# Fused attention and expert layers on one core: the second token group's first expert products as 2x2 blocks with seven block products

## The chip, the cores and the metric

One core of one Trainium2 chip runs the whole program. The metric is the device time of one execution in microseconds (us), a median over runs. Engine names are those of the profile: PE is TensorE's matmul, PEld its weight load, DVE is VectorE, ACT is ScalarE, POOL is GpSimd, SP is SyncE, whose queue issues nearly all DMAs.

## The reference, cut to what matters

```python
x = attention(q, k, v, tau)                       # 2 x 576 tokens, 8 heads of 64: 1152 x 512
h = np.maximum(np.maximum(x @ w1, x @ w2), x @ w3) # "max" layer, 512 -> 768
x = h @ w_out                                      # 768 -> 512
p = domain_probs / (domain_probs.sum(-1, keepdims=True) + 1e-09)
for e in range(4):                                 # every token goes through every expert
    h = np.maximum(x @ w1[e], 0.0)                 # first expert product, 512 -> 1024
    out += p[:, e:e + 1] * (h @ w2[e])             # second expert product, 1024 -> 512
```

All is float32. The kernel works each product from two-part values: every operand is cut into a high part (rounded to the type that PE multiplies quickly) and a low part (the rest), and a product is the sum of three matmuls, high x low, low x high and high x high.

## The kernel before, in words

The 1152 tokens are two groups: group 0 has 512 tokens, group 1 has 640 (`GROUPS`, line 78), the latter worked as two halves of 320 columns (`subs`). For each group `layer_max` (line 723) runs the max layer and the output product, then `experts` (line 793) the four experts. Both only plan: `add` (line 719) appends a task, which is one PSUM tile, its chain of matmuls, and the functions that read the tile afterwards. `plan.cols` counts the matmul columns planned so far; it is the clock of the plan.

`Stream.run` (line 852) writes the plan out. It issues the matmuls of the tasks one after the other (the matmul is line 859 for all of them), taking the PSUM tile from the pool `mo["ps"]`, which has 3 banks. The readers of a task go out 1000, 2000, ... columns after its end (`AFTER`, line 862). Weight loads and cuts are hooks, put in with `plan.at` at a number of columns ahead of their use (their lag); `flush` (line 843) writes out whatever is due, late functions and hooks in the order of their columns. In the last two regions of the program the order on PE, DVE, ACT and POOL is just this written order (`ORDER_B`, `ORDER_C`), so every engine takes its instructions strictly in turn; that of SP is left to the scheduler.

In the stage of the change, `experts(1)`, each expert is done in two halves of four hidden blocks of 128 (so eight halves). For each block f, `block` (line 644) loads a 128 x 512 weight tile (line 658, 256 KB), cuts its high part on ACT (line 650) and its low part on POOL (line 654). Two tasks (one per 320-column half of the tokens) follow, each of 4 chunks of the 512 inputs times three matmuls; the readers are `hi` (ACT, line 809: relu and rounding) and `lo` (DVE, line 812: relu less the high part, from PSUM). Then five tasks, one per 128 tokens, do the second product: 4 hidden blocks times three matmuls of 512 columns, and `total` (DVE, line 828; line 826 for the first) adds p times the result to the accumulator. The last half stores it (line 786).

The output product of `layer_max(1)` just before makes the inputs `Y[1][d]` (d = 0 to 3, high and low), with `hi` on ACT (line 768) and `lo` on DVE (line 771); for each d the left half of the tokens comes ahead of the right.

Between the groups, at the column count `END0`, group 0's last readers are written out, the pools of the second attention half are closed, and new pools for group 1's hidden tiles and accumulators are opened (lines 959 to 965). The three PSUM banks go on being used.

Of the kernel before, what the change touches and what calls it, by code (L numbers as in the profile page):

```python
# [21 lines left out]
def fused_kernel(ctx: ExitStack, tc: tile.TileContext, q, k, v, tau, w1, w2, w3, w_out, probs, m_w1, m_w2, out):  # L22
    nc = tc.nc
    B, H, S, D = q.shape
    NT, DM = out.shape
    DFF = w1.shape[1]
    E, _, F2 = m_w1.shape
    P = 128
# [6 lines left out]
    KC = DM // P  # L35
# [36 lines left out]
    def f32(ap):  # L72
        return ap.bitcast(F32)
# [3 lines left out]
    N1 = NT - MAIN  # L77
# [2 lines left out]
    cst = ctx.enter_context(tc.tile_pool(name="cst", bufs=1))  # L80
    wp = ctx.enter_context(tc.tile_pool(name="wp", bufs=1))
    dp = ctx.enter_context(tc.tile_pool(name="dp", bufs=1, space=bass.MemoryType.DRAM))
    with tc.using_default_side("right"):
        xp1 = ctx.enter_context(tc.tile_pool(name="xp1", bufs=1))
        xp0 = ctx.enter_context(tc.tile_pool(name="xp0", bufs=1))

    ident = cst.tile([P, P], F32, name="ident")
    make_identity(nc, ident)
# [12 lines left out]
    Y = [[None] * KC for _ in range(2)]  # L101
# [12 lines left out]
    def atile(shape, dt, tag):  # L114
        return at["pool"].tile(shape, dt, tag=tag, name=tag, bufs=at["bufs"].get(tag, 1))
# [337 lines left out]
    class Queue:  # L453
# [3 lines left out]
        def add(self, gen):  # L457
            self.q.append(gen)
# [183 lines left out]
    plan = Plan()  # L642
# [80 lines left out]
    def layer_max(g):  # L723

        G = GROUPS[g]
        hs = [None] * NF
        acc = {}

        def after_max(f, i, si, a, z):
            def first(ps):  # L730
                if hs[f] is None:
                    hs[f] = (htile(g, "hh"), htile(g, "hl"))
                new = wtile([P, z - a], F32, "hmax", 3)
                if i == 0:
# [24 lines left out]
        for d in range(KC):  # L759
            bs = []  # L760
            for i in range(2):
                src = block64(w_out[i * K2 * P:(i + 1) * K2 * P], slice(d * P, (d + 1) * P))
                bs.append(weights64(g, f"o{d}_{i}", plan.cols + i * 3 * K2 * G["subs"][0][1], src, [P, K2, P]))
            for a, z in G["subs"]:
                def hi(ps, d=d, a=a, z=z):
                    if Y[g][d] is None:
                        Y[g][d] = tuple((xp0, xp1)[g].tile([P, G["n"]], F32R, tag="xy", name=f"y{g}{part}{d}", bufs=2 * KC) for part in "hl")
                    nc.scalar.activation(out=Y[g][d][0][:, a:z], in_=ps, func=AF.Copy)

                def lo(ps, d=d, a=a, z=z):  # L770
# [22 lines left out]
    def experts(g):  # L793

        G = GROUPS[g]
        FH = NF2 // 2
        nt = G["n"] // P
        accs = {}
        for e in range(E):
            for half in range(2):  # L800
                hs = [None] * FH
                for f in range(FH):
                    c0 = (half * FH + f) * P
                    b = block(plan.cols, [P, KC, P], "a", NA, None, lags(G, LAGS_A[e + half > 0][f]), src=m_w1[e, :, c0:c0 + P].rearrange("(k p) f -> p k f", p=P))
# [12 lines left out]
                ws = []  # L817
                for f in range(FH):
                    r0 = (half * FH + f) * P
                    ws.append(block(plan.cols, [P, DM], "b", NB, None, lags(G, LAGS_B[f]), src=m_w2[e, r0:r0 + P, :]))  # L820
                for t in range(nt):
                    def total(ps, t=t, e=e, half=half):
                        pe = pr[:, G["c0"] + t, e:e + 1]
                        if e == 0 and half == 0:
                            accs[t] = mo["acc"].tile([P, DM], F32, tag="acc", name="acc", bufs=nt)
                            nc.vector.tensor_scalar(out=accs[t], in0=ps, scalar1=pe, scalar2=None, op0=ALU.mult)
                        else:
                            nc.vector.scalar_tensor_tensor(out=accs[t], in0=ps, scalar=pe, in1=accs[t], op0=ALU.mult, op1=ALU.add)  # L828
# [4 lines left out]
                    add(DM, FH, lambda f, ts=ts, hs=hs, ws=ws: (  # L833
                        hs[f][0][:, ts], hs[f][1][:, ts], ws[f]["hi"], ws[f]["lo"]), [total])

    class Stream:

# [93 lines left out]
        pass  # L931
    stage.close()

    def open_experts(name, side):
        with tc.using_default_side(side):
            mo["h"] = ctx.enter_context(tc.tile_pool(name=f"hp{name}", bufs=1))
            mo["acc"] = ctx.enter_context(tc.tile_pool(name=f"accp{name}", bufs=1))

    region.close()
    region = ordered(ORDER_B)  # L940
    mo["ps"] = ctx.enter_context(tc.tile_pool(name="psM", bufs=3, space=PSUM))
    mo["bits"] = words_pool.enter_context(tc.tile_pool(name="bitsp", bufs=2, space=PSUM))
    open_experts(0, "right")
    while stream.now < QUE0:
        next(products)
    for before, until in (("turned", QUE1), ("valued", QUE2)):
# [52 lines left out]
```

## Time and profile before, and how to read it

| what | value |
|---|---|
| median of 3 runs | 738.38 us (738.06 to 738.91) |
| the profiled execution | 738.01 us, of which the span from first to last instruction is 736.2 us |
| PE busy | 707.0 us of the span |
| POOL, DVE, ACT busy | 377.2, 379.6, 324.8 us |
| instructions | 11651, of them 4047 matmuls |
| mean granted clock | 0.995 of full speed |

Busy time of PE is not its peak: matmuls are pipelined, so a matmul that is shown with 0.31 us may start 0.15 us after the one before. The distance from start to start tells what one costs. "Idle before" is the time in which an engine had nothing running, and the arrow behind it names what ended it.

### The profile page before, as it was taken

Reading aid. Unit: us, or ns where it says so; the run is one execution under the profiler, and the core shown is the slowest. Engines: PE = TensorE matmul, PEld = TensorE weight load, DVE = VectorE, ACT = ScalarE, POOL = GpSimd, SP = SyncE. Lnnn points to the kernel's source line nnn. Section 1 sums busy time; section 2 is a strip of 40 time slices with the busy share of each in tenths; the row PEclk is TensorE's granted clock in tenths of the full one; section 3 lists DMA queues with packets and bytes.
Section 4 is the critical chain, followed back from the end, with each engine's and each line's share of the span. In section 5 each row is a group of like instructions: output and inputs, shape, how many; then the busy total and the mean of one; then the engine's idle time right before and its main releaser. Section 6 shows DMA issues by size and latency. Waiting matters only on the chain.

```text
span 736.2 us, 11651 instructions
## 1 busy us (share of the span) xinstructions
PE 707.0 (96%) x4047; PEld 629.3 (85%) x4047; DVE 379.6 (52%) x907; ACT 324.8 (44%) x681; POOL 377.2 (51%) x394
## 2 busy tenths in 40 slices
PE   5988899999999999999999999999999999999997
PEld 3877789777888888878888899999998998998995
DVE  6898898775476676666676311212222222222222
ACT  5777875544554564454454323234331321322320
POOL 4778876776563564564465344455423423523520
PEclk9899999999999999999999999999999999999999
DMA  6644606877766246153222322224412312312303
GB/s 185 156 96 103 181 1 193 268 220 223 195 164 167 72 109 163 58 135 104 60 85 58 115 76 72 76 66 115 115 49 66 115 46 70 115 44 71 115 1 71
DMA packets 95150, 80.86 MB, mean 110 GB/s; under 512 B 26356, under 2 KB 75764, under 8 KB 95092
## 3 DMA queue, kind: packets, MB, share of 16 engines
q1 hardware_dynamic: 94642, 79.83, 39.9%
q8 instruction: 32, 0.52, 0.3%
q10 hardware_dynamic: 418, 0.30, 0.2%
q14 instruction: 26, 0.21, 0.1%
q0 software_dynamic: 32, 0.00, 0.0%
HBM read 59.53 MB, written 8.65 MB: 93 GB/s over the span
## 4 chain that ended last, share of the span: by engine, by line
PE 80%; DVE 7%; ACT 3%; POOL 3%; issue 3%; DMA 2%; SPq 0%; DVEq 0%; ACTq 0%; POOLq 0%
PE ps L859 67%; PE u L434 4%; PE s L317 4%; PE t L358 3%; DVE em L340 2%; DMA words<-in_moe_w_dram 1%; POOL a L654 1%; DVE st_negm L328 1%; ACT em L335 1%; POOL b L683 1%; DMA krem<-in_k_dram 1%; DVE raw L691 1%; POOL hl L745 1%; DVE hmax L737 1%; ACT a L650 1%
## 5 line engine op out<-in xcount | busy, mean ns | idle before, releaser
L654 POOL TENSOR_TENSOR a<-raw,a 128x512 fp32r<-128x512 f32 (+1 forms) x116 | 145.1, 1257 | 170.5 <-ACT a L650 162.5
L859 PE MATMUL ps<-b,hh 128*128 128x512 f32 x576 | 184.9, 393 | 0.0
L859 PEld LDWEIGHTS ps<-b,hh 128*128 128x128 f32 x576 | 107.4, 188 | 20.8 <-POOL b L654 0.4
L859 PE MATMUL ps<-b,hl 128*128 128x512 f32 x288 | 113.1, 393 | 0.0
L859 PE MATMUL ps<-y1h,a 128*128 128x320 f32 x512 | 112.8, 309 | 0.0
L809 ACT ACTIVATE hh<-ps 128x320 fp32r<-128x320 f32 (+1 forms) x96 | 46.9, 488 | 147.1 <-PE ps L859 146.8
L654 POOL TENSOR_TENSOR b<-raw,b 128x512 fp32r<-128x512 f32 x64 | 82.9, 1296 | 56.2 <-ACT b L650 56.2
L812 DVE SCALAR_TENSOR_TENSOR hl<-ps,hh 128x320 fp32r<-128x320 f32 (+1 forms) x96 | 53.5, 557 | 102.6 <-ACT hh L809 102.4
L650 ACT ACTIVATE a<-raw 128x512 fp32r<-128x512 f32 (+1 forms) x116 | 69.5, 612 | 66.7 <-DVE raw L691 20.7
L828 DVE SCALAR_TENSOR_TENSOR acc<-ps,pr,acc 128x512 f32<-128x512 f32 x63 | 47.2, 749 | 77.7 <-PE ps L859 77.5
L859 PEld LDWEIGHTS ps<-y1h,a 128*128 128x128 f32 x512 | 85.4, 188 | 0.3
L859 PE MATMUL ps<-y0h,a 128*128 128x512 f32 x256 | 84.1, 399 | 0.0
L335 ACT ACTIVATE em<-s,st_negm 128x576 f32<-128x576 f32 x72 | 53.4, 743 | 68.9 <-DVE st_negm L328 66.2
L348 POOL TENSOR_SCALAR em<-em,st_r,even 128x576 f32<-128x576 f32 x70 | 57.7, 825 | 48.2 <-DVE st_r L347 34.2
L859 PE MATMUL ps<-y1l,a 128*128 128x320 f32 x256 | 79.1, 309 | 0.0
L328 DVE TENSOR_REDUCE st_negm<-s 128x1 f32<-128x576 f32 x72 | 54.2, 754 | 45.7 <-PE s L317 45.6
L859 PE MATMUL ps<-x1h,a 128*128 128x320 f32 x288 | 63.4, 309 | 0.0
L859 PEld LDWEIGHTS ps<-b,hl 128*128 128x128 f32 x288 | 54.1, 188 | 10.0
L340 DVE SCALAR_TENSOR_TENSOR em<-s,st_thr,em 128x576 f32<-128x576 f32 x72 | 58.4, 812 | 6.6 <-ACT em L335 4.4
L317 PE MATMUL s<-K,QS 128*128 128x288 f32 x264 | 49.8, 313 | 7.4 <-DVE em L340 6.9
L859 PEld LDWEIGHTS ps<-y0h,a 128*128 128x128 f32 x256 | 47.3, 189 | 8.4
L317 PEld LDWEIGHTS s<-K,QS 128*128 128x128 f32 x264 | 41.9, 197 | 12.8 <-issue 5.7
(128 smaller groups left out, 1241.5 us busy)
## 6 DMA issues: line engine op xcount, KB each, us to landing
raw<-in_moe_w_dram SPq DMA_DIRECT2D x128, 256.0 KB, 2.8
words<-in_moe_w_dram SPq DMA_DIRECT2D x18, 512.0 KB, 6.2
kept_w<-raw SPq DMA_DIRECT2D x18, 256.0 KB, 2.5
raw<-kept_w SPq DMA_DIRECT2D x18, 256.0 KB, 2.6
K<-KN SPq DMA_DIRECT2D x14, 288.0 KB, 5.0
K<-KN SPq DMA_DIRECT2D x14, 256.0 KB, 3.5
words<-in_moe_w_out_dram SPq DMA_DIRECT2D x8, 384.0 KB, 4.9
vnat<-in_v_dram SPq DMA_DIRECT2D x8, 256.0 KB, 4.4
```

Of the source, the lines that this page charges most:

```text
L317: nc.tensor.matmul(st.s[:, kh, 0:HS], lhsT=l, rhs=r, start=i == 0, stop=i == len(terms) - 1)
L328: nc.vector.tensor_reduce(out=st.stat["negm"], in_=views(st)[0], op=ALU.max, axis=AX.XY, negate=True)
L335: return nc.scalar.activation(out=ev, in_=sv, func=AF.Exp, bias=st.stat["negm"])
L340: nc.vector.scalar_tensor_tensor(out=ev, in0=sv, scalar=st.stat["thr"], in1=ev, op0=ALU.is_ge, op1=ALU.mult, accum_out=st.stat["sum"])
L348: last = (nc.vector if swift else nc.gpsimd).tensor_scalar(out=em, in0=em, scalar1=re, scalar2=even, op0=ALU.mult, op1=ALU.add)
L434: at["valued"] = nc.tensor.matmul(pv, lhsT=l, rhs=r, start=i == 0, stop=i == len(terms) - 1)
L650: nc.scalar.activation(out=b["hi"], in_=b["raw"], func=AF.Copy)
L654: nc.gpsimd.tensor_tensor(out=b["lo"], in0=b["raw"], in1=f32(b["hi"]), op=ALU.subtract)
L809: nc.scalar.activation(out=hs[f][0][:, a:z], in_=ps, func=AF.Relu)
L812: nc.vector.scalar_tensor_tensor(out=hs[f][1][:, a:z], in0=ps, scalar=0.0, in1=f32(hs[f][0][:, a:z]), op0=ALU.max, op1=ALU.subtract)
L828: nc.vector.scalar_tensor_tensor(out=accs[t], in0=ps, scalar=pe, in1=accs[t], op0=ALU.mult, op1=ALU.add)
L859: nc.tensor.matmul(ps, lhsT=l, rhs=r, start=i == 0, stop=i == count - 1)
```

## The change

The eight block products of each pair of hidden blocks become seven. The inputs are split into a low half (d = 0, 1) and a high half (d = 2, 3), the pair of hidden blocks into two, the tokens into left and right: a 2x2 by 2x2 block product, done in Winograd's form of Strassen's method. It needs four sums of weight blocks and four sums of input blocks.

- Input sums (`mixed_values`): the readers of the output product of `layer_max(1)` also make the four mixed inputs `BT`, high and low, on DVE and ACT. For d = 2 and 3 the right half of the tokens now comes first.
- Weight sums (`pair_block`): one load of 512 KB per pair takes the place of two of 256 KB. Four sums on DVE (two functions, `sums` and `sums2`), three cuts on ACT and three on POOL, each with its own lag. The buffers are doubled.
- Products (`mixed_pair`): seven tasks per pair, each of 2 chunks times three matmuls of 320 columns. Their readers add the seven results up on DVE, and then do relu, high and low. For two of the four outputs ("calm") relu and high are on ACT and low is on POOL.
- The second products take the token tiles in the order 4 to 0, and the hidden blocks as 0, 1, 3, 2.
- Pools: group 0's input pool and its hidden, accumulator and PSUM pools are closed at `END0`; group 1 gets a new PSUM pool of 8 banks and a pool `mixp`.

```diff
+    group0 = ExitStack()
...
-        xp0 = ctx.enter_context(tc.tile_pool(name="xp0", bufs=1))
+        xp0 = group0.enter_context(tc.tile_pool(name="xp0", bufs=1))
...
-            for a, z in G["subs"]:
+            for a, z in G["subs"] if d < KC // 2 else G["subs"][::-1]:
...
-                    bs[j // K2]["hi"][:, j % K2, :], bs[j // K2]["lo"][:, j % K2, :], hs[j][0][:, a:z], hs[j][1][:, a:z]), [hi, lo])
+                    bs[j // K2]["hi"][:, j % K2, :], bs[j // K2]["lo"][:, j % K2, :], hs[j][0][:, a:z], hs[j][1][:, a:z]),
+                    [hi, lo] if g == 0 else mixed_values(d, a > 0, hi, lo))
...
+    def mixed_values(d, right, hi, lo):
...
+        y0, y1, t2, t3 = (lambda nm=nm, x=x: whole(nm)[:, x, :] for nm in "yt" for x in range(2))
+        if low and not right:
+            return [hi, lo, keep(0)]
+        if low:
+            return [less(y0, y0), *cut(0, y0), keep(1)]
+        if right:
+            return [less(y0, t2), less(y1, t3), *cut(1, t2), *cut(2, t3), hi, lo]
+        return [less(t2, t2), *cut(3, t2), hi, lo]
+
+    def pair_block(use, src, lags):
...
+            b["raw"] = mo["mix"].tile([P, KC, 2 * P], F32, tag="wraw", name="wraw", bufs=2)
+            nc.sync.dma_start(out=b["raw"], in_=src)
...
+            nc.vector.tensor_tensor(out=S(0), in0=raw(1, 0), in1=raw(1, 1), op=ALU.add)
+            nc.vector.tensor_tensor(out=S(2), in0=raw(0, 0), in1=raw(1, 0), op=ALU.subtract)
...
+            nc.vector.tensor_tensor(out=S(1), in0=S(0), in1=raw(0, 0), op=ALU.subtract)
+            nc.vector.tensor_tensor(out=S(3), in0=raw(0, 1), in1=S(1), op=ALU.subtract)
...
+        for fn, lag in zip((load, sums, sums2, hi, shi(0), shi(2), lo, slo(0), slo(2)), lags):
+            plan.at(use - lag, fn)
...
+    LAGS_PAIR = (
+        (44000, 30000, 29000, 28000, 27000, 26000, 26500, 24000, 21500),
+        (44000, 29000, 28000, 27000, 26000, 25000, 24000, 21500, 18500))
+
+    def mixed_pair(b, hs, f):
...
+            def lo(ps):
+                if calm:
+                    nc.gpsimd.tensor_tensor(out=hs[f + i][1][:, cols], in0=val[nm], in1=f32(hs[f + i][0][:, cols]), op=ALU.subtract)
+                else:
+                    nc.vector.scalar_tensor_tensor(
+                        out=hs[f + i][1][:, cols], in0=val[nm], scalar=0.0, in1=f32(hs[f + i][0][:, cols]), op0=ALU.max, op1=ALU.subtract)
...
+        for w, y, after in (
+                (lambda: d(0), direct(0, left), [copy("cx")]),
+                (lambda: s(0), mixed(0), [keep("p5")]),
+                (lambda: s(1), mixed(1), [plus("cu", "cx"), plus("cv", "cu", "p5")]),
+                (lambda: s(2), mixed(2), [plus("cw", "cv"), plus("cu", "cu"), *act(1, right, "cw", True)]),
+                (lambda: d(1), direct(1, left), [plus("cx", "cx"), *act(0, left, "cx", True)]),
+                (lambda: s(3), direct(1, right), [plus("cv", "cv"), *act(0, right, "cv")]),
+                (lambda: d(2), mixed(3), [plus("cu", "cu"), *act(1, left, "cu")])):
+            add(TH, KC // 2, lambda j, w=w, y=y: tuple(t[:, j, :] for t in w()) + tuple(y(j)), after)
...
-                for f in range(FH):
+                for f in range(0, FH, 2) if g == 1 else ():
+                    c0 = (half * FH + f) * P
+                    b = pair_block(plan.cols, m_w1[e, :, c0:c0 + 2 * P].rearrange("(k p) f -> p k f", p=P), LAGS_PAIR[f // 2])
+                    mixed_pair(b, hs, f)
+                for f in range(FH) if g == 0 else ():
...
-                for t in range(nt):
+                for t in range(nt)[::1 if g == 0 else -1]:
...
+                    add(DM, FH, lambda i, ts=ts, hs=hs, ws=ws, order=(0, 1, 2, 3) if g == 0 else (0, 1, 3, 2): (
...
-    open_experts(1, "left")
+    group0.close()
+    open_experts(1, "left", ctx)
+    mo["ps"] = ctx.enter_context(tc.tile_pool(name="psN", bufs=8, space=PSUM))
+    mo["mix"] = ctx.enter_context(tc.tile_pool(name="mixp", bufs=1))
```

## Rows read from the trace of the kernel before

**Rows 1.** The chain that ended last, its last pieces: start us, us, what.

```profile
413.18 318.36 PE ps L859 x1878
731.54 0.02 issue
731.56 0.75 DVE acc L828
```

**Rows 2.** Busy time by stretch: max layer of group 1, its experts, one half of these.

```profile
core 0: us, PE busy (x) PEld busy (x) DVE busy (x) ACT busy (x) POOL busy (x), PEclk, DMA share, GB/s
425.10:509.76 84.66, 84.66 (x579) 84.62 (x578) 16.00 (x32) 27.38 (x58) 40.91 (x38) 1.00 0.26 76
509.76:731.54 221.78, 221.76 (x1250) 202.53 (x1248) 61.24 (x104) 60.23 (x126) 80.25 (x63) 1.00 0.27 75
537.50:565.20 27.70, 27.70 (x158) 25.34 (x157) 7.69 (x13) 7.77 (x16) 10.25 (x8) 1.00 0.26 76
```

**Rows 3.** The timeline of the first expert task's end: start us, us, what.

```profile
511.08 0.31 PE L859 MATMUL ps<-y1l,a 128*128 128x320 f32 x1
511.22 0.46 PE L859 MATMUL ps<-y1h,a 128*128 128x320 f32 x2
511.52 0.31 PE L859 MATMUL ps<-y1l,a 128*128 128x320 f32 x1
511.72 0.44 ACT L809 ACTIVATE hh<-ps 128x320 fp32r<-128x320 f32 x1 [0.80 <-PE ps L859]
```

**Rows 4.** The timeline of group 0's last matmuls and of what follows them.

```profile
424.15 0.39 PE L859 MATMUL ps<-b,hl 128*128 128x512 f32 x1
424.37 0.62 PE L859 MATMUL ps<-b,hh 128*128 128x512 f32 x2
424.83 0.39 PE L859 MATMUL ps<-b,hl 128*128 128x512 f32 x1
425.28 0.30 PE L859 MATMUL ps<-x1l,a 128*128 128x320 f32 x1
425.48 0.75 DVE L828 SCALAR_TENSOR_TENSOR acc<-ps,pr,acc 128x512 f32<-128x512 f32 x1 [1.97 <-PE ps L859]
```

**Rows 5.** Groups by line and shape, 509.76 to 731.54: xcount | busy us, mean ns | idle before.

```profile
L859 PE MATMUL ps<-y1h,a 128*128 128x320 f32 x512 | 112.8, 309 | 0.0
L859 PE MATMUL ps<-y1l,a 128*128 128x320 f32 x256 | 79.1, 309 | 0.0
L654 POOL TENSOR_TENSOR b<-raw,b 128x512 fp32r<-128x512 f32 x32 | 41.6, 1301 | 28.5 <-ACT b L650 28.5
L654 POOL TENSOR_TENSOR a<-raw,a 128x512 fp32r<-128x512 f32 x31 | 39.5, 1294 | 100.5 <-ACT a L650 100.5
L812 DVE SCALAR_TENSOR_TENSOR hl<-ps,hh 128x320 fp32r<-128x320 f32 x64 | 31.5, 492 | 82.6 <-ACT hh L809 82.6
L809 ACT ACTIVATE hh<-ps 128x320 fp32r<-128x320 f32 x64 | 27.8, 435 | 137.5 <-PE ps L859 137.5
L828 DVE SCALAR_TENSOR_TENSOR acc<-ps,pr,acc 128x512 f32<-128x512 f32 x34 | 25.5, 751 | 65.7 <-PE ps L859 65.7
L650 ACT ACTIVATE a<-raw 128x512 fp32r<-128x512 f32 x30 | 17.3, 626 | 9.8 <-PE ps L859 9.8
```

**Rows 6.** Groups by shape on DVE and POOL, whole span: other shapes.

```profile
L218 DVE TENSOR_TENSOR em<-qnat,em 128x256 f32<-128x256 f32 x2 | 0.8, 419 | 0.0
L745 POOL TENSOR_TENSOR hl<-hmax,hh 128x320 fp32r<-128x320 f32 x12 | 10.6, 880 | 22.1 <-ACT hh L742 22.1
L451 POOL TENSOR_TENSOR x0l<-x,x0h 128x256 fp32r<-128x256 f32 x7 | 5.2, 737 | 0.5 <-ACT x0h L448 0.4
L654 POOL TENSOR_TENSOR a<-raw,a 128x384 fp32r<-128x384 f32 x16 | 16.3, 1019 | 14.5 <-ACT a L650 14.4
```

**Rows 7.** The timeline near 105 us: a DVE and a POOL instruction, both on SBUF.

```profile
103.89 1.28 POOL L409 TENSOR_TENSOR am<-tcopy,am 128x512 fp32r<-128x512 f32 x1
104.98 0.58 DVE L348 TENSOR_SCALAR em<-em,st_r,even 128x576 f32<-128x576 f32 x1
```

**Rows 8.** DMA issues: xcount, KB each, median us from issue to landing.

```profile
raw<-in_moe_w_dram SPq DMA_DIRECT2D x128, 256.0 KB, 2.8
words<-in_moe_w_dram SPq DMA_DIRECT2D x18, 512.0 KB, 6.2
```

More of the change, by code (lines that the diff above doesn't have):

```diff
@@ L773, in layer_max, with part, whole, keep @@
                 add(z - a, NF, lambda j, bs=bs, a=a, z=z: (
-                    bs[j // K2]["hi"][:, j % K2, :], bs[j // K2]["lo"][:, j % K2, :], hs[j][0][:, a:z], hs[j][1][:, a:z]), [hi, lo])
+                    bs[j // K2]["hi"][:, j % K2, :], bs[j // K2]["lo"][:, j % K2, :], hs[j][0][:, a:z], hs[j][1][:, a:z]),
+                    [hi, lo] if g == 0 else mixed_values(d, a > 0, hi, lo))
+    TH = N1 // 2
+    BT = [[None] * KC for _ in range(4)]
+    full = {}
+    def mixed_values(d, right, hi, lo):
+        low, c = d < KC // 2, d % (KC // 2)
+        def part(x):
+            BT[x][c] = tuple(mo["mix"].tile([P, TH], F32R, tag="bt", name=f"bt{y}{x}{c}", bufs=4 * KC) for y in "hl")
+            return BT[x][c]
+        def whole(nm):
+            if (nm, c) not in full:
+                full[nm, c] = f32(htile(1, "y32"))[:, 0:2 * TH].rearrange("p (x t) -> p x t", x=2)
+            return full[nm, c]
+        def keep(x):
+            return lambda ps: nc.scalar.activation(out=whole("y")[:, x, :], in_=ps, func=AF.Copy)
+        def less(x, to):
+            return lambda ps: nc.vector.tensor_tensor(out=to(), in0=ps, in1=x(), op=ALU.subtract)
+        def cut(x, src):
+            def hi(ps):
+                part(x)
+                nc.scalar.activation(out=BT[x][c][0], in_=src(), func=AF.Copy)
+            def lo(ps):
+                nc.vector.tensor_tensor(out=BT[x][c][1], in0=src(), in1=f32(BT[x][c][0]), op=ALU.subtract)
+            return [hi, lo]
+        y0, y1, t2, t3 = (lambda nm=nm, x=x: whole(nm)[:, x, :] for nm in "yt" for x in range(2))
[6 more added lines that the diff above has]
+        return [less(t2, t2), *cut(3, t2), hi, lo]
@@ new lines, in pair_block, with load, sums, sums2 @@
+    def pair_block(use, src, lags):
+        b = {}
+        raw = lambda i, j: b["raw"][:, 2 * j:2 * j + 2, i * P:(i + 1) * P]
+        S = lambda x: b["s"][:, x, :, :]
+        def load():
+            b["raw"] = mo["mix"].tile([P, KC, 2 * P], F32, tag="wraw", name="wraw", bufs=2)
+            nc.sync.dma_start(out=b["raw"], in_=src)
+        def sums():
+            b["s"] = mo["mix"].tile([P, 4, 2, P], F32, tag="s", name="s", bufs=2)
+            nc.vector.tensor_tensor(out=S(0), in0=raw(1, 0), in1=raw(1, 1), op=ALU.add)
+            nc.vector.tensor_tensor(out=S(2), in0=raw(0, 0), in1=raw(1, 0), op=ALU.subtract)
+        def sums2():
+            nc.vector.tensor_tensor(out=S(1), in0=S(0), in1=raw(0, 0), op=ALU.subtract)
+            nc.vector.tensor_tensor(out=S(3), in0=raw(0, 1), in1=S(1), op=ALU.subtract)
+        def pieces():
+            return (b["raw"][:, :, 0:P], slice(0, 2)), (raw(1, 1), slice(2, 3))
+        def rows(t, x):
+            return t[:, x].rearrange("p a b f -> p (a b) f")
+        def hi():
+            b["dh"] = mo["mix"].tile([P, 3, 2, P], F32R, tag="dh", name="dh", bufs=2)
+            for src, x in pieces():
+                nc.scalar.activation(out=rows(b["dh"], x), in_=src, func=AF.Copy)
+        def lo():
+            b["dl"] = mo["mix"].tile([P, 3, 2, P], F32R, tag="dl", name="dl", bufs=2)
+            for src, x in pieces():
+                nc.gpsimd.tensor_tensor(out=rows(b["dl"], x), in0=src, in1=f32(rows(b["dh"], x)), op=ALU.subtract)
+        def shi(x):
+            def fn():
+                if x == 0:
+                    b["sh"] = mo["mix"].tile([P, 4, 2, P], F32R, tag="sh", name="sh", bufs=2)
+                nc.scalar.activation(out=rows(b["sh"], slice(x, x + 2)), in_=rows(b["s"], slice(x, x + 2)), func=AF.Copy)
+            return fn
+        def slo(x):
+            def fn():
+                if x == 0:
+                    b["sl"] = mo["mix"].tile([P, 4, 2, P], F32R, tag="sl", name="sl", bufs=2)
+                nc.gpsimd.tensor_tensor(
+                    out=rows(b["sl"], slice(x, x + 2)), in0=rows(b["s"], slice(x, x + 2)),
+                    in1=f32(rows(b["sh"], slice(x, x + 2))), op=ALU.subtract)
+            return fn
+        for fn, lag in zip((load, sums, sums2, hi, shi(0), shi(2), lo, slo(0), slo(2)), lags):
+            plan.at(use - lag, fn)
+        return b
@@ new lines, in fused_kernel, with keep, temp, copy @@
+    LAGS_PAIR = (
+        (44000, 30000, 29000, 28000, 27000, 26000, 26500, 24000, 21500),
+        (44000, 29000, 28000, 27000, 26000, 25000, 24000, 21500, 18500))
+    def mixed_pair(b, hs, f):
+        Yg = Y[1]
+        left, right = slice(0, TH), slice(TH, 2 * TH)
+        d, s = (lambda x: (b["dh"][:, x], b["dl"][:, x])), (lambda x: (b["sh"][:, x], b["sl"][:, x]))
+        direct = lambda x, cols: lambda j: tuple(t[:, cols] for t in Yg[2 * x + j])
+        mixed = lambda x: lambda j: BT[x][j]
+        val = {}
+        def keep(nm):
+            return lambda ps: val.update({nm: ps})
+        def temp(nm):
+            val[nm] = mo["mix"].tile([P, TH], F32, tag=nm, name=nm, bufs=2)
+            return val[nm]
+        def copy(nm):
+            return lambda ps: nc.scalar.activation(out=temp(nm), in_=ps, func=AF.Copy)
+        def plus(out, x, y=None):
+            def fn(ps):
+                add1 = val[x]
+                nc.vector.tensor_tensor(
+                    out=val[out] if out in val else temp(out), in0=val[y] if y else ps, in1=add1, op=ALU.add)
+            return fn
+        def act(i, cols, nm, calm=False):
+            def relu(ps):
+                nc.scalar.activation(out=val[nm], in_=val[nm], func=AF.Relu)
+            def hi(ps):
+                if hs[f + i] is None:
+                    hs[f + i] = (htile(1, "hh"), htile(1, "hl"))
+                nc.scalar.activation(out=hs[f + i][0][:, cols], in_=val[nm], func=AF.Relu)
+            def lo(ps):
+                if calm:
[3 more added lines that the diff above has]
+                        out=hs[f + i][1][:, cols], in0=val[nm], scalar=0.0, in1=f32(hs[f + i][0][:, cols]), op0=ALU.max, op1=ALU.subtract)
+            return [relu, hi, lo] if calm else [hi, lo]
+        for w, y, after in (
[7 more added lines that the diff above has]
+            add(TH, KC // 2, lambda j, w=w, y=y: tuple(t[:, j, :] for t in w()) + tuple(y(j)), after)
@@ L932, in fused_kernel, with open_experts @@
     stage.close()
[L934 removed]
+    def open_experts(name, side, held):
         with tc.using_default_side(side):
[L936 to L937 removed]
+            mo["h"] = held.enter_context(tc.tile_pool(name=f"hp{name}", bufs=1))
+            mo["acc"] = held.enter_context(tc.tile_pool(name=f"accp{name}", bufs=1))
     region.close()
     region = ordered(ORDER_B)
[L941 removed]
+    mo["ps"] = group0.enter_context(tc.tile_pool(name="psM", bufs=3, space=PSUM))
     mo["bits"] = words_pool.enter_context(tc.tile_pool(name="bitsp", bufs=2, space=PSUM))
[L943 removed]
+    open_experts(0, "right", group0)
     while stream.now < QUE0:
```

3 lines of the change are left out of this document (1 added, 2 removed).

## The prediction

> **What bounds the kernel now.** I read the chain that ended last first. Its last 318.36 us are one piece, the product matmuls without a break, then 0.02 us and one accumulation on DVE [rows 1]. So from 413 us on nothing but PE sets the end, and the changed stage lies inside. The busy time by stretch says the same: in group 1's experts PE is busy 221.76 of 221.78 us at full granted clock, while DVE, ACT and POOL are busy 61.24, 60.23 and 80.25 us [rows 2]. One half of an expert takes 27.70 us, with 7.69 us of DVE, 7.77 of ACT and 10.25 of POOL.
>
> Next, what a matmul costs there. Three 320-column matmuls take 511.52 - 511.08 = 0.44 us from start to start, 146.7 ns each [rows 3]; the 309 ns in their group row is the time of one in the pipeline, not its price. Three of 512 columns take 424.83 - 424.15 = 0.68 us, 226.7 ns each [rows 4]. Check: the stage has 512 + 256 = 768 matmuls of 320 columns [rows 5] and, by the code, 480 of 512: 768 x 0.1467 + 480 x 0.2267 = 221.5 us, against 221.78 [rows 2].
>
> A measurement of this kernel can tell about 0.2% (1.5 us) from no change.
>
> **What is removed.** A pair of hidden blocks has eight block products of 6 matmuls now, seven after. There are 16 pairs, so 16 x 6 = 96 matmuls of 320 columns go: 96 x 146.7 ns = **14.08 us**, all of it on the chain. PE's work per half falls from 27.70 to 84 x 0.1467 + 60 x 0.2267 = 25.92 us. Whether it is earned depends on the other engines, which get more to do.
>
> **What is added, per half (two pairs).**
> - POOL, per pair: a cut of 512 elements (1.294 us) and one of 256 (0.737), two more of 512 for the sums (2.59), two calm lows of 320 (2 x 0.880) = 6.38 [rows 5, 6]. Twice that and four `b` cuts of 1.301 make 17.97 us of 25.92 (69%), from 10.25.
> - DVE, per pair: four sums of 256 elements (4 x 0.419, the only row of that shape whose inputs both lie in SBUF), seven additions at 0.492, two lows at about the same = 6.10 us [rows 5, 6]. Twice that and five totals of 0.751 make 15.96 us (62%), from 7.69.
> - ACT, per pair: three cuts of 512 (0.626) and one of 256 (about 0.37, by the slope from 320 to 512), one copy, two relus and four highs at 0.435 = 5.29 [rows 5]. With four `b` cuts 13.1 us (51%), from 7.77.
>
> No engine becomes the bound by its sum. What can cost is a value that is late in a strict queue, so I followed the deadlines by the columns of the plan (0.458 us per 1000).
>
> **Weights.** `sums` is planned 30000 columns ahead of use and the last low 21500 (18500 for the second pair), 9.8 (8.5) us. POOL's cuts of one pair take 4.6 us. Ahead of the very first pair they share POOL with cuts for the output product (1.019 us each [rows 6]): two of these, then 4.6 us, then two more, planned from 29540 columns ahead, make 8.7 us and end 0.7 us or more ahead of each need. Cost 0; if POOL were late there, it would be once, under 1 us. The SP queue gets simpler, two loads of 512 KB for four of 256 per half.
>
> **Inputs.** The mixed inputs cost DVE about 16 x 0.49 = 8 us and ACT about 5 us in a stretch where they are busy 16.00 and 27.38 of 84.66 us [rows 2]. The last to be ready, after the final output task, is a chain of four DVE and two ACT steps, some 2.2 us; the pair's first product that needs one of its results comes 3.5 us (four tasks of 0.88) after. Cost 0. Moving the right half first for d = 2, 3 gives the other mixed inputs 2.64 us more.
>
> **From the pair to the second product.** This is the tight place, once per half. The first token tile (t = 4) takes hidden blocks 0, 1, 3, 2. The low part of block 2's right half comes from the sixth product and is first needed by the 11th matmul of that tile: 10 x 0.2267 = 2.27 us after the seventh product's last matmul was issued (call that 0). A result can be read 0.20 us after its task [rows 3]. By the columns, DVE takes in this order: the addition of product 6 (-0.68 to -0.19), the next pair's two `sums` (0.84 us, to 0.65), the addition of product 7 (to 1.14), then the low in question (to 1.63). Slack 0.64 us. Block 3's right half is a calm one, done on POOL near -0.15 and needed at 7 x 0.2267 = 1.59. Cost 0 if these durations hold.
>
> **The change of groups.** The new PSUM pool takes all eight banks, hence also the one that group 0's last total reads until 425.48 + 0.75 = 426.23, while group 1's first matmul now starts at 425.28 [rows 4]. If the first tile waits only for its own bank, it costs 0; if for all the old tiles, 1.0 us. Nothing in the trace shows which; the pools as wholes are closed and opened here, so I take 1.0 and keep 0 for the low end.
>
> **The order at the end** (t = 0 last) leaves one total and its stores after the last matmul, as now [rows 1]: 0. The three PSUM banks that become eight only loosen.
>
> **Sum** against the profiled execution: 738.01 - 14.08 + 1.0 = 724.9 us. The median of the runs lies 0.37 us above that execution, so **725.3 us**.
>
> **Rival 1: DVE and POOL in each other's way.** In the trace a DVE instruction with one SBUF tensor ran wholly inside a POOL subtraction, 104.98 to 105.56 in 103.89 to 105.17, and neither took longer than its like [rows 7]. No row shows POOL against a DVE instruction with two tensors from SBUF; the sums and lows are such. Suppose they exclude each other. The first `sums` then waits for the calm low of product 4 (to -0.15), the calm low of product 5 (0.880) gets in between the two and holds the second until 1.15, and the low needed at 2.27 ends near 2.6. PE stops some 0.33 us in each of the seven halves that prepare a next one: 2.3 us, so **727.6**. If DVE waits twice for a whole calm low, 1.63 + 1.76 = 3.39, it is 1.1 us a half, 7.8 us, 733. [...] In capacity even exclusion fits: 17.97 us of POOL and 8 x 0.419 + 4 x 0.49 = 5.3 of DVE are 23.3 of 25.92.
>
> **Rival 2, on the other side: the 512 KB load comes late.** `sums` stands in DVE's queue ahead of product 7's addition. If the load has not landed, DVE stands still, the additions behind it too, and PE waits for the hidden block. The load is planned 14000 columns, 6.4 us, ahead of `sums`; the 512 KB loads of the trace landed in a median 6.2 us, the 256 KB ones in 2.8 [rows 8]. With the 0.64 us of slack it costs nothing up to 7.1 us. Slower than before by 1.5 us needs 14.08 - 1.0 + 1.5 = 14.6 us over seven halves, 2.1 each: landings of 9.2 us. At 10 us it would be 725.3 + 7 x 2.9 = **745.6**. Against it: DMA engines are busy only 0.27 here [rows 2], and the buffer (two) comes free long before, so that SP can issue early.
>
> **Rival 3: fewer matmuls, no gain,** because the distance between matmuls grows (new operands) or the stalls happen to eat it: 96 x 146.7 ns spread over the 672 of 320 columns that remain is 21 ns each. Nothing speaks for it; the distance is the same for every operand in rows 3 and in the sum above. That the change doesn't do what it says is excluded by the code: seven tasks of 2 chunks.
>
> **How the numbers follow.** Forecast (no stall but the change of groups, 724 to 726) 0.58; rival 1 with 726 to 733 0.31; rival 2 0.08; rival 3 0.03. Low end: no wait at the groups, 724.3, less half the spread of the runs, 723.7. High end: rival 1 with 0.9 us in each of seven halves, 731.5. Left out are rival 1's worst, rivals 2 and 3. Faster by over 0.2%: 0.90; within: 0.02; slower: 0.08.
>
> **What would show it.** 3951 matmuls on the page; the experts' stretch near 207.4 us (8 x 25.92) with PE busy throughout and 320-column distances of 146.7 ns; about 18 us of POOL and 16 of DVE per half. The wait at the groups: a first `x1l` matmul that starts after DVE's last total. Rival 1: PE idle before a 512-column matmul that ends on DVE's low, and sums or calm lows that take visibly longer than 0.419 and 0.880. Rival 2: DVE idle ended by the load. The prediction is wrong if PE is idle over 8 us in all, or if the chain leaves PE.

## The result and the profile after

The changed kernel takes 730.35 us (median of 4 runs, 730.02 to 730.89), the kernel before beside it 738.64 (738.06 to 739.36). The ratio is 0.9888, 95% interval 0.9871 to 0.9905: 8.3 us faster. A second comparison of the same two on another chip, given below, has 0.9873 (0.9857 to 0.9889), 9.2 us. The forecast was 725.3 us in a range of 723.7 to 731.5.

The profiled execution takes 730.22 us with a span of 728.4. PE runs 3951 matmuls, 96 fewer. The chain that ended last, from the change of groups on (start us, us, what; pieces of the middle left out), is to be set beside [rows 1]:

```profile
415.03 12.28 PE ps L1020 x54
427.31 0.03 issue
427.33 0.76 DVE acc L989
428.23 72.39 PE ps L1020 x492
500.63 0.39 issue
501.01 0.53 ACT a L651
...
511.38 1.00 DVE btl L809 x2
512.38 1.36 issue
513.74 0.49 DVE y L801
...
519.81 203.84 PE ps L1020 x1125
723.65 0.03 issue
723.67 0.75 DVE acc L989
```

Before, the last 318 us were one piece of PE. Now the chain leaves PE at the change of groups (427.31) and for 19 us, from 500.63 to 519.81, at the step from the max layer to the experts. From there it is one piece to the end. The view of the waits on PE, 405 to 736 us, gives the same four places (who waited for whom, us in total, times, longest); before it had no line there:

```profile
PE ps L1020 <- DVE btl L809: 1.2, 1, 1.2
PE ps L1020 <- DVE acc L989: 0.9, 1, 0.9
PE ps L1020 <- POOL a L655: 0.7, 1, 0.7
PE ps L1020 <- DVE y1l L772: 0.5, 1, 0.5
```

The timeline shows each as a gap between matmuls. Counted from start to start, over 146.7 or 226.7 ns, and with the matmul behind it, which starts late too, they are 1.17 us (the max layer's first matmul, 428.23), 1.00 (a matmul of the output product, 508.55), 1.44 (the first pair's third product, 517.33) and 0.73 (its fifth, 519.81): 4.35 us. Three of them:

```profile
507.51 0.31 PE L1020 MATMUL ps<-hl,a 128*128 128x320 f32 x1
508.55 0.56 PE L1020 MATMUL ps<-hh,a 128*128 128x320 f32 x2 [0.73 <-POOL a L655]
517.33 0.41 PE L1020 MATMUL ps<-btl,sh 128*128 128x320 f32 x1 [1.18 <-DVE btl L809]
519.04 0.31 PE L1020 MATMUL ps<-y1h,dh 128*128 128x320 f32 x1
519.81 0.42 PE L1020 MATMUL ps<-y1l,dh 128*128 128x320 f32 x1 [0.46 <-DVE y1l L772]
```

One half of the experts, by stretch, beside the last of [rows 2], with the same columns:

```profile
541.89:567.83 25.94, 25.94 (x145) 23.58 (x144) 20.33 (x31) 11.92 (x26) 19.25 (x17) 1.00 0.28 82
```

25.94 us, where 25.92 had been worked out, and PE without a gap. DVE is busy 20.33 us and not 15.96, POOL 19.25 and not 17.97. Why is in the groups by shape from 520 to 724 us:

```profile
L854 POOL TENSOR_TENSOR dl<-wraw,dh 128x512 fp32r<-128x512 f32 x14 | 20.6, 1472 | 0.0
L918 DVE SCALAR_TENSOR_TENSOR hl<-cu,hh 128x320 fp32r<-128x320 f32 x16 | 17.6, 1102 | 0.0
L918 DVE SCALAR_TENSOR_TENSOR hl<-cv,hh 128x320 fp32r<-128x320 f32 x16 | 10.1, 629 | 2.0 <-ACT hh L912 1.1
L837 DVE TENSOR_TENSOR s<-s,wraw 128x256 f32<-128x256 f32 x14 | 14.4, 1028 | 0.0
L833 DVE TENSOR_TENSOR s<-wraw 128x256 f32<-128x256 f32 x14 | 12.2, 872 | 0.0
L901 DVE TENSOR_TENSOR cv<-ps,cu 128x320 f32<-128x320 f32 x16 | 7.9, 492 | 0.5
```

The sums (L833 to L838) and the lows (L918) read two tensors from SBUF. The sums take more than twice the 419 ns of [rows 6], from 415 up to 1511 ns apiece, and the lows 1102 and 629 ns where 490 had been assumed. The additions (L901), which read one tensor from PSUM, take 492 ns as ever. POOL's cuts grow as well (1472 for 1294).

The account of the profiled executions: -14.08 for the matmuls, +4.35 for the stops, and +1.86 ahead of the change of groups, where group 0's last matmul starts at 426.91 us and not at 425.05 [rows 4]. The sum is -7.87, against 730.22 - 738.01 = -7.79. The 1.86 us are the first thing to explain, since in the two traces every compute engine runs the same instructions in the same order up to there.

### The profile page after: what moved, and what is told of

It is laid out like the page before. It is cut to its first block, busy times and chain, and to the rows that moved or that the text cites. A ratio compares the mean times of both kernels' runs of the same rounds, so it can differ in the third digit from the quotient of the medians.

```text
span 728.4 us, 11799 instructions
## 1 busy us (share of the span) xinstructions
PE 696.0 (96%) x3951; PEld 617.0 (85%) x3951; DVE 488.3 (67%) x1065; ACT 362.0 (50%) x771; POOL 449.5 (62%) x458
## 4 chain that ended last, share of the span: by engine, by line
PE 78%; DVE 8%; ACT 4%; issue 3%; POOL 3%; DMA 1%; SPq 0%; DVEq 0%; POOLq 0%; ACTq 0%
PE ps L1020 64%; PE u L435 4%; PE s L318 4%; PE t L359 3%; DVE em L341 2%; POOL a L655 1%; DVE st_negm L329 1%; ACT em L336 1%; DMA krem<-in_k_dram 1%; POOL b L684 1%; DVE raw L692 1%; ACT a L651 1%; POOL hl L746 1%; DMA words<-in_moe_w_dram 1%; PE t L405 1%
## 5 line engine op out<-in xcount | busy, mean ns | idle before, releaser
L655 POOL TENSOR_TENSOR a<-raw,a 128x512 fp32r<-128x512 f32 (+1 forms) x84 | 104.7, 1248 | 66.7 <-ACT a L651 63.4
L651 ACT ACTIVATE a<-raw 128x512 fp32r<-128x512 f32 (+1 forms) x84 | 50.8, 606 | 52.0 <-DVE raw L692 17.6
L738 DVE TENSOR_TENSOR hmax<-ps,hmax 128x320 f32<-128x320 f32 (+2 forms) x38 | 20.3, 535 | 53.4 <-PE ps L1020 52.7
L1020 PE MATMUL ps<-y0l,a 128*128 128x512 f32 x128 | 51.0, 398 | 0.0
L1020 PEld LDWEIGHTS ps<-x1h,a 128*128 128x128 f32 x288 | 48.2, 188 | 0.0
L1020 PE MATMUL ps<-x0h,a 128*128 128x512 f32 (+1 forms) x168 | 46.3, 362 | 1.8 <-POOL a L655 1.8
L867 POOL TENSOR_TENSOR sl<-s,sh 128x512 fp32r<-128x512 f32 x32 | 43.2, 1369 | 7.6 <-ACT sh L860 7.6
```

Source lines behind the costliest of these rows:

```text
L651: nc.scalar.activation(out=b["hi"], in_=b["raw"], func=AF.Copy)
L655: nc.gpsimd.tensor_tensor(out=b["lo"], in0=b["raw"], in1=f32(b["hi"]), op=ALU.subtract)
L867: nc.gpsimd.tensor_tensor(out=rows(b["sl"], slice(x, x + 2)), in0=rows(b["s"], slice(x, x + 2)), in1=f32(rows(b["sh"], slice(x, x + 2))), ...
L1020: nc.tensor.matmul(ps, lhsT=l, rhs=r, start=i == 0, stop=i == count - 1)
```

## The experiments

**The kernel before again** (no edit).

> The kernel before once more, for the stretch up to the change of groups, in which the changed kernel issues the same instructions in the same order on every compute engine and yet came 1.85 us later. If that is the ordinary scatter from one execution to the next (when the granted clock falls early in the program), the first matmul of group 1, at 425.28 us in the first profile, lies up to 2 us off here too. If the change causes it, it lies within 0.2 us of 425.28.

Measured: 739.4 us, span 737.6; group 0's last matmul starts at 426.42 us and group 1's first at 426.64, 1.36 us later than in the first profile of the same kernel. Over all profiles of this study group 0's last matmul starts between 424.38 and 427.52 us: 425.05 and 426.42 in the kernel before, 426.91 and 427.31 in the changed kernel, the two ends in edited versions of it. It is scatter between executions; a cost of the change of a few tenths there can't be excluded.

**Group 0's banks not given on.**

```diff
-    mo["ps"] = group0.enter_context(tc.tile_pool(name="psM", bufs=3, space=PSUM))
+    mo["ps"] = ctx.enter_context(tc.tile_pool(name="psM", bufs=3, space=PSUM))
...
-    mo["ps"] = ctx.enter_context(tc.tile_pool(name="psN", bufs=8, space=PSUM))
+    mo["ps"] = ctx.enter_context(tc.tile_pool(name="psN", bufs=5, space=PSUM))
```

> Group 0's three PSUM banks stay with their pool, and group 1 takes the five others, so that no bank that group 0's last total still reads is given on. Theory: the 1.17 us without matmuls at the change of groups are the wait for that total; they go, and 1.2 us of the span with them, while the three later stops (1.0, 1.44 and 0.73 us) stay. Rival: the stop is the opening of the new hidden-tile pools, or of any new PSUM pool; then it stays at about 1.1 us.

Measured: 726.76 us, one run. In this kernel's timeline group 1 starts 0.22 us after group 0's last matmul, while the last total still has to begin:

```profile
424.38 0.39 PE L1020 MATMUL ps<-b,hh 128*128 128x512 f32 x1
424.60 0.30 PE L1020 MATMUL ps<-x1l,a 128*128 128x320 f32 x1
424.81 0.75 DVE L989 SCALAR_TENSOR_TENSOR acc<-ps,pr,acc 128x512 f32<-128x512 f32 x1 [1.97 <-PE ps L1020]
```

The stop was the wait for that total, by the first tile of the new pool. New pools are opened here too, without a stop, so the rival is out. The stops at the output product (1.0 us) and at the first pair (2.2 us in all) stay. (The single time profits from an early group 0, the 424.38.)

**The first two pairs' weights earlier.**

```diff
-                    b = pair_block(plan.cols, ..., LAGS_PAIR[f // 2])
+                    b = pair_block(plan.cols, ..., tuple(x + (EARLIER if e + half == 0 else 0) for x in LAGS_PAIR[f // 2]))
...
+    EARLIER = 50000
```

> The weight preparation of the first two pairs alone (load, sums, cuts) is put 50000 columns (23 us) earlier, out of the stretch in which the input sums are made. Theory: the three stops between 508 and 520 us (3.17 us) come from that crowd, two-input instructions on DVE and POOL's cuts holding each other up; they fall to 0.3 us or less in all and the time to about 727.3. Rival: the chain of input sums after the last output tasks is too long by itself; then the stops at the pair's third and fifth product (1.44 and 0.73) stay, only the 1.0 us before them goes, and the time is about 729.4.

Measured: 726.73 us (725.26 to 727.79, 4 runs) against 738.76; ratio 0.9841 (0.9819 to 0.9862). All three stops before and in the first pair are gone, but for 0.2 us near 487 where the work went; the one at the change of groups stays. The chain after the change of groups is one piece up to the last total:

```profile
426.65 292.48 PE ps L1022 x1728
```

The input sums by themselves are not late; the crowd was.

**Which pair.** The same, with `and f == 2` added to the condition: the second pair alone.

> Only the second pair's preparation is put 50000 columns earlier, the first pair's is left. Theory: the stop at the third product (1.44 us) and that at the fifth (0.73) come from the second pair's sums, and from POOL's cuts of it holding up the lows of the inputs, since these lie between 506.5 and 515 us; both fall to 0.3 us or less. The 1.0 us before them, POOL's late cut for the output product, comes from the first pair's cuts and stays. Rival: the first pair's preparation is enough to make DVE late; then 0.5 us or more is left of the two.

Measured: 728.39 us, one run. The stops at the third and fifth product are gone, the one before them is 1.07 us with the matmul behind it (508.83). So the second pair's preparation made DVE late, and the first pair's made POOL late. No run moved the first pair alone.

**Sums that read one SBUF tensor.**

```diff
-            nc.vector.tensor_tensor(out=S(0), in0=raw(1, 0), in1=raw(1, 1), op=ALU.add)
+            nc.vector.tensor_scalar(out=S(0), in0=raw(1, 0), scalar1=pr[:, 0, 0:1], scalar2=pr[:, 0, 1:2], op0=ALU.mult, op1=ALU.add)
```

(and likewise the other three)

> The four weight sums of each pair are made by an instruction that reads one SBUF tensor instead of two (one block scaled and shifted; the sums are left out of the computation). Theory, that a DVE instruction with two SBUF inputs and a POOL instruction exclude each other: these four fall from 0.87 to 1.03 us on average to 0.35 to 0.45 whatever POOL does, POOL's cuts of the pair's blocks from 1.472 to near 1.3, while DVE's lows, which still read two, stay at 0.6 to 1.1. Rival, that DVE is slow there for the reading of strided blocks or because loads land in the same stretch: the sums stay near 0.9. The stop at the pair's third product shrinks by 0.5 us or more under the theory.

A miss. Measured: 727.97 us; from 520 to 724 us the four take 0.655 to 0.894 us on average, not 0.35 to 0.45; POOL's cut of 512 takes 1.342, as expected; the stop at the third product is 1.07 us with the matmul behind it, 0.4 less. Either the exclusion was wrong, or the form that I had put in is itself one that POOL excludes. The cost had to be measured alone.

**Five forms of a DVE instruction, with and without POOL.** Core of the kernel:

```python
two:  nc.vector.tensor_tensor(out=x, in0=A, in1=B, op=ALU.add)            # L42
onep: nc.vector.tensor_tensor(out=x, in0=ps, in1=B, op=ALU.add)           # L45
scal: nc.vector.tensor_scalar(out=x, in0=A, scalar1=sc[:, 0:1], scalar2=sc[:, 1:2], op0=ALU.mult, op1=ALU.add)  # L48
imm:  nc.vector.tensor_scalar(out=x, in0=A, scalar1=1.5, scalar2=0.5, op0=ALU.mult, op1=ALU.add)                # L51
stt:  nc.vector.scalar_tensor_tensor(out=x, in0=ps, scalar=sc[:, 0:1], in1=B, op0=ALU.mult, op1=ALU.add)        # L54
```

> The disputed cost by itself; nothing of the reference is computed. Five forms of a 256-element DVE instruction, twelve of each, first with POOL idle, then while POOL runs 128x512 subtractions without a break: two SBUF tensors added; a PSUM and an SBUF tensor added; one SBUF tensor times and plus two scalars that are read from SBUF (the form of the run in which the sums were replaced); the same with constants; a PSUM tensor times a scalar from SBUF plus an SBUF tensor (the form of the totals). Theory: alone all take 0.3 to 0.45 us. Beside POOL the first grows to 1.2 us or more, since it has to wait for POOL's instruction to end, and POOL's 1.29 grows by about 0.4 where it has to wait in turn; the second and the fifth stay as they were. The replaced sums stayed slow (0.66 to 0.89), so the third and the fourth have to grow as well if that run is to be understood. Rival, that landings or strided blocks made the sums slow: none of the five changes beside POOL.

Measured. Each form's minimum, median and maximum in ns, over 12 alone and 12 beside POOL:

```profile
L42 DVE TENSOR_TENSOR o<-wide x24: 412/415/425, 4.4 to 27.5; 128x256 f32<-128x256 f32 x24
L45 DVE TENSOR_TENSOR o<-psA,wide x24: 410/410/414, 8.4 to 31.4; 128x256 f32<-128x256 f32 x24
L48 DVE TENSOR_SCALAR o<-wide,sc x24: 401/726/1348, 12.4 to 45.4; 128x256 f32<-128x256 f32 x24
L51 DVE TENSOR_SCALAR o<-wide x24: 281/814/1345, 16.2 to 60.6; 128x256 f32<-128x256 f32 x24
L54 DVE SCALAR_TENSOR_TENSOR o<-psA,sc,wide x24: 468/471/474, 18.7 to 66.2; 128x256 f32<-128x256 f32 x24
```

The two `tensor_scalar` forms take 401 and 281 ns alone and about 1345 beside POOL: each waits for a whole POOL subtraction. So the replacement in the run above was excluded too, and that run says nothing against the theory. The two forms with a PSUM operand don't change. The first, two SBUF tensors, seems not to change either, against what I expected, but the timeline shows who paid:

```profile
23.76 4.10 DVE L42 TENSOR_TENSOR o<-wide 128x256 f32<-128x256 f32 x12
23.93 11.28 POOL L63 TENSOR_TENSOR g<-go,r 128x512 f32<-128x512 f32 x6 [23.48 <-DVE go L61]
27.79 4.06 DVE L45 TENSOR_TENSOR o<-psA,wide 128x256 f32<-128x256 f32 x12
```

The six POOL subtractions that begin at 23.93 take 11.28 us; five of them take their usual 1.26 to 1.31. The first took 5.07 us: it stood until DVE's twelve additions were over at about 27.8 us and ran while DVE read from PSUM. The twelve came first and back to back, and POOL did not get in between. So POOL and DVE in these forms keep each other out, and the one that holds on makes the other wait. For the two-tensor form this rests on a single POOL instruction, the first of its kind there, but it ends 1.2 us after DVE passed on to the next form, which is its usual time. The expected price for POOL did not come: beside the `tensor_scalar` forms its subtractions start 1.267 us apart, and beside a DVE that reads PSUM 1.225. How the DVE instruction fits into the 0.04 us between stays open.

The Trainium skill, SBUF — State Buffer, section "Who interferes with whom", says that the one that issues first gets the shared ports for its whole instruction, and lists `tensor_scalar` among the forms that can take them, on conditions for its operands. The 1345 ns agree with the second. On the first the row goes further: POOL was held off for twelve instructions, not for one.

**The sums with one operand in PSUM.** ACT copies three of the four blocks there.

```diff
+        def staged():
+            b["p1"] = mo["st"].tile([P, 2, 2 * P], F32, tag="p1", name="p1", bufs=1)
+            b["p2"] = mo["st"].tile([P, 2, P], F32, tag="p2", name="p2", bufs=1)
+            nc.scalar.activation(out=b["p1"], in_=b["raw"][:, 0:2, :], func=AF.Copy)
+            nc.scalar.activation(out=b["p2"], in_=raw(0, 1), func=AF.Copy)
...
-            nc.vector.tensor_tensor(out=S(0), in0=raw(1, 0), in1=raw(1, 1), op=ALU.add)
+            nc.vector.tensor_tensor(out=S(0), in0=b["p1"][:, :, P:2 * P], in1=raw(1, 1), op=ALU.add)
...
+        plan.at(use - lags[1] - 1000, staged)
```

> ACT copies three of the four weight blocks of each pair into PSUM first, and each of the four sums then reads one operand from there (PSUM pool of 6 banks instead of 8). Theory, that two tensors read from SBUF are what POOL and DVE cannot do together: the four sums fall from 0.87 to 1.03 us to 0.42 +- 0.05, without scatter, and POOL's cuts of the pair's blocks from 1.472 to 1.35 or less; the stop at the pair's third product shrinks from 1.44 by 0.5 us or more; the time falls by 0.5 to 1.5 us. Rival, as above: the sums stay near 0.9.

Measured: 732.28 us, one run. The sums are flat, medians from 410 to 424 ns; the first of the four (minimum, median, maximum):

```profile
L839 DVE TENSOR_TENSOR s<-p,wraw x16: 414/423/425, 499.2 to 692.1; 128x256 f32<-128x256 f32 x16
```

That is the theory's number; in the changed kernel it ranged from 415 to 1335 ns. The blocks are as strided and the loads land as before, so the rival is out. POOL's cut of the sums is back at 1.289 us, but the one of 512 elements stays at 1.469, not 1.35 or less: a DVE low with two SBUF tensors lies beside it. The stop at the third product shrank to 0.5 us, as expected. The time did not fall, though: each of the seven halves that prepare a next one now has a stop of 0.3 to 0.65 us at the 11th matmul of its second product (3.4 us in all with the matmuls behind them), because ACT's two copies stand ahead of the high part that is due there, and the sums on DVE wait for them. The place that I had called tight is tight: its slack was 0.7 us (below).

**Token tiles and hidden blocks in the old order.**

```diff
-                for t in range(nt)[::1 if g == 0 else -1]:
+                for t in range(nt):
...
-order=(0, 1, 2, 3) if g == 0 else (0, 1, 3, 2)
+order=(0, 1, 2, 3)
```

> The second products take token tiles and hidden blocks in their old order again (0 to 4; 0, 1, 2, 3). The low part of the last block's left half, which ended 4.97 us after the seventh product in the half looked at, is then needed by the first tile's 11th matmul, 2.27 us after it. Theory: the order is what keeps the eight halves free of stops; without it PE stops 2.0 to 3.0 us in seven halves and less in the last (which prepares no next pair), 15 to 22 us in all, about 748 us: the whole gain is gone. Rival: the halves have slack enough in any order, the time stays within 3 us of 730.

Measured: 760.77 us, one run; more than expected. From group 0's last matmul to the last of all, 34.1 us are lost beyond the matmuls' distances at full clock. Seven halves have a stop of 0.73 us for POOL's low and one of 1.84 for DVE's, 18.0 us in all, as expected, and 19.5 with the matmuls behind them; the eighth half loses 0.8. The rest, beyond the 4.4 of the changed kernel, is 9.4 us of a lower clock (busy time by stretch, columns as in [rows 2], the clock third from the end):

```profile
531.00:534.00 3.00, 1.09 (x4) 0.61 (x4) 2.79 (x3) 1.81 (x5) 3.00 (x4) 0.89 0.00 0
534.00:537.00 3.00, 3.00 (x8) 2.38 (x9) 0.75 (x1) 0.38 (x2) 3.00 (x3) 0.54 0.55 175
```

From 531 to 534 us PE was busy 1.09 of 3.00 us and stood still twice. In the next 3 us the granted clock was 0.54, mostly the lower level of 1.2 GHz, and the matmuls of 512 columns came 427 ns apart instead of 227, until the clock was whole again near 537. It fell in six of the seven halves, during the second stop or within a microsecond of it; in the fifth the same two stops left it at 1.00.

**Both repairs together**, the banks and the earlier weights.

> Both repairs: group 0's PSUM banks are not given on, and the first two pairs' weights are prepared 50000 columns earlier. Theory: no stop is left from the change of groups to the end, so all of the 14.08 us is kept: 738.7 - 14.1 = 724.6 us, within 0.7. Rival: taking the stops away shows the next late thing behind them, 726 or more.

Measured: 725.88 us (724.97 to 726.35, 5 runs) against 739.65; ratio 0.9812 (0.9796 to 0.9829), 13.8 us faster. The kernel before was 0.9 us slower on this chip than on the last, which is where the absolute time went past the expectation. From 414.51 us to the last total the chain is PE but for 0.01 us (0.28 us counted as above, at 486.77):

```profile
414.51 72.25 PE ps L1022 x463
486.76 0.01 issue
486.77 232.29 PE ps L1022 x1319
```

Nothing else was late behind the stops. From group 0's last matmul to the last of all it takes 292.27 us, where the kernel before takes 306.08: 13.81 us less, which is the 14.08 of the seven products less the 0.28. This version beats both kernels; its ratio's interval lies below that of the changed kernel.

**The changed kernel again** (no edit).

> The changed kernel once more. By its stops it should gain 14.08 - 4.35 = 9.7 us; its first comparison gave 8.3. If the rest is scatter of the early stretch from execution to execution, the median of these five lies 9.7 +- 0.8 us below the kernel before on the same chip, and the first matmul of group 1 comes at another time than 428.23 us. If the changed kernel has a cost of its own ahead of the change of groups, the difference stays at 8.3 and that matmul near 428.2.

Measured: 730.25 us (729.19 to 731.03, 5 runs) against 739.43; 9.2 us less, ratio 0.9873 (0.9857 to 0.9889), so within the expectation of 9.7 +- 0.8. But group 1's first matmul starts at 428.63 us, close to the 428.23 of the first profile. The gain agrees with the stops. In these profiles the stretch behind the change of groups doesn't scatter: from group 0's last matmul to the last of all, both profiles of the kernel before take 306.08 us and both of the changed kernel 296.34, which is 9.74 us less. The two measured gains miss 1.4 and 0.5 us of that, and these lie outside of the stretch; whether a few tenths ahead of it belong to the change stays open.

## Why the prediction was right or wrong

The sign, and the place of the gain, were right: 96 matmuls at 146.7 ns, a half at 25.94 us for 25.92, no gap behind the first pair of the eight halves, and 13.8 of the 14.08 us once the stops are taken out. The time is 5 us above the forecast but in the range. Of these, 3.2 are stops that I had priced at nothing, 0.2 the change of groups, and the rest lies ahead of it, where executions scatter. That the time lies in the range at all is luck: the upper end was set by rival 1's stops in seven halves, and none of these came. (The lower end should have read 723.9: half the spread of the runs is 0.4 us.) Of the two signs of being wrong that the prediction names, one came: from the change of groups on PE lost 4.35 us and not 8, but the chain did leave PE, for 19 us ahead of the experts.

**The change of groups.** Taken at 1.0 us, measured 1.17. The run with separate banks shows that the first tile waits for the last total because the banks are given on. Whether it waits for all of the old pool's tiles, as I had assumed, or happens to get the very bank of that total, no run tells apart.

**Inputs, "cost 0": this step failed.** It put DVE's work at 8 us among 16 busy of 84.66 us, and the last chain at 2.2 us with 1.3 to spare. The chain by itself is sized well: in the run with both pairs' weights earlier, its last low is ready 2.37 us after the final output task (513.80 and 511.43 us). Wrong was that DVE is free when the chain starts. The second pair's sums and cuts fall into the same 12 us, which I had counted under Weights only, and there the two-input instructions and POOL's cuts hold each other up. In the timeline of the changed kernel:

```profile
509.62 2.35 POOL L854 TENSOR_TENSOR dl<-wraw,dh 128x512 fp32r<-128x512 f32 x2
509.97 1.40 DVE L838 TENSOR_TENSOR s<-wraw,s 128x256 f32<-128x256 f32 x1
511.30 2.52 DVE L809 TENSOR_TENSOR btl<-y,bth 128x320 fp32r<-128x320 f32 x2
511.93 3.05 POOL L867 TENSOR_TENSOR sl<-s,sh 128x512 fp32r<-128x512 f32 x2
513.74 0.48 DVE L801 TENSOR_TENSOR y<-ps,y 128x320 f32<-128x320 f32 x1
515.65 0.87 DVE L801 TENSOR_TENSOR y<-ps,y 128x320 f32<-128x320 f32 x2
519.26 0.49 DVE L772 TENSOR_TENSOR y1l<-ps,y1h 128x320 fp32r<-128x320 f32 x1 [0.16 <-ACT y1h L769]
```

A sum takes 1.40 us and two lows 2.52, each beside a POOL cut, and DVE falls behind. The subtraction at 513.74 belongs to the third output task from the end, whose matmuls were through at 507.5; the two at 515.65 belong to the last but one, through at 511.1. The last low is ready at 519.75, 5.97 us after the final output task (513.79) and not 2.2. So the third product's input is ready at 517.3, 1.4 us late, and the fifth's 0.7. The run with only the second pair moved away takes both stops out.

**Weights, "cost 0; under 1 us if POOL were late".** POOL was late, by 1.0 us, the bound. My 0.7 us of margin had been worked out from undisturbed durations, and from 499.37 to 509.66 us POOL's cuts take 9.55 us where I had added up 8.7. It also stands idle for 1.00 us (to 501.61): by the profile it waits there for a cut on ACT, and that one for the POOL cut before, which had taken 1.25 us instead of 1.02.

**Rival 1 had the mechanism and not the place.** I had given it seven stops of 0.33 us between pair and second product. There the durations do grow, but nothing stops. The timeline of one half says why (the second product's first matmul starts at 554.21, which is the 0 of the prediction):

```profile
553.94 0.41 DVE L833 TENSOR_TENSOR s<-wraw 128x256 f32<-128x256 f32 x1
554.21 0.39 PE L1020 MATMUL ps<-b,hh 128*128 128x512 f32 x1
554.27 0.42 DVE L834 TENSOR_TENSOR s<-wraw 128x256 f32<-128x256 f32 x1
554.34 1.08 POOL L916 TENSOR_TENSOR hl<-cw,hh 128x320 fp32r<-128x320 f32 x1 [1.42 <-ACT hh L912]
555.02 0.75 DVE L918 SCALAR_TENSOR_TENSOR hl<-cv,hh 128x320 fp32r<-128x320 f32 x1
```

The sums are near where I had put them (-0.27 and 0.06, for -0.19 and 0.23), but the calm low comes at +0.13, not at -1.03: its high part stands on ACT behind the relu of the other calm output, which waits for the fifth product. Both sums get through ahead of POOL. The low in question ends at 555.77, 0.71 us ahead of its need at 556.48; I had worked out 0.64, and it is 0.70 or more in every half. I had not foreseen that order on ACT, so the forecast of no stop here came true partly by luck. The rival's worst case was not reached; the two runs that disturbed this place lost 0.3 to 0.65 us and 2.6 us per half there.

**My reading of [rows 7] was wrong.** I took the DVE instruction for one that ran wholly inside POOL's. It ends at 105.56, 0.39 us after POOL's (105.17), so only 0.19 of its 0.58 us lie inside. The five forms show that a `tensor_scalar` with one SBUF tensor waits for POOL. The row alone doesn't show that, but it was no evidence against exclusion, and without it rival 1 would have had a higher chance.

**Rival 2.** The 512 KB loads landed in a median 3.4 us, and no idle time of DVE ahead of a sum ended with one: not that. **Rival 3:** the distances are 146.7 and 226.7 ns as before.

## What to carry to other kernels

An edit that gives idle engines more work can cost, as here, where the work of two stages meets; a margin there has to be worked out with all that both stages issue, not stage by stage, and with durations beside a busy neighbour. The work that starts a new stage can sometimes be done much earlier at little cost: here, put 23 us earlier into a stretch with room, it took 3.2 us of stops away and left 0.2 to 0.3. Leave memory that the last reader still needs to its old pool if there is other room: a reused PSUM pool cost 1.2 us, three banks left alone cost nothing.

## What the runs showed of the hardware

In these float32 runs DVE and POOL's subtractions in SBUF held each other up where DVE read two SBUF tensors, and in `tensor_scalar` on one: 401 and 281 ns alone became 1345 beside POOL, while a row of twelve two-tensor additions made one POOL instruction take 5.07 us. A PSUM operand instead of one SBUF tensor avoided it (410 and 470 ns, unchanged; the four sums 410 to 424). In the run with the old order the granted clock fell to its lower level during or just behind the second of two stops, of 0.73 and 1.84 us, in six halves of seven; in the changed kernel, with two stops of 1.44 and 0.73 us as close together, it stayed at 1.00. These falls cost 9.4 us beside the 19.5 of the stops: a wait can cost more than its own length.
